# Step 4's outputs in products of 256 columns, value groups around the first new memories, and the first loads on another queue

## The chip, the cores and the metric

The kernel runs on one core of one Trainium2 chip. The metric is the device time of one execution in microseconds (us), taken as the median over runs; before the change it is 1577.51 us (three runs, 1575.53 to 1577.84). A core has engines that run side by side, each with its own instruction stream: PE (TensorE) multiplies matrices, DVE (VectorE), ACT (ScalarE) and POOL (GpSimd) work on elements, SP (SyncE) only starts transfers here. ACT and POOL can start transfers too. PE, DVE, ACT and POOL work on on-chip memory (SBUF); PE writes into accumulators (PSUM), which DVE and ACT copy out ("evict").

## The reference

Two kinds of layer, A and B, alternate twice over x, one sequence of 2048 tokens of 512 numbers:

```python
x = x + A(layernorm(x));  x = x + B(layernorm(x))
x = x + A(layernorm(x));  x = x + B(layernorm(x))

def A(x):                                # weights in bf16, 32 heads of 128
    mem = mem0                           # 8 rows of 512
    for s in range(64):                  # segments of 32 tokens
        h = concat(mem, x[32 * s: 32 * s + 32])          # 40 rows
        q, k, v = h @ Wq, h @ Wk, h @ Wv                 # per head
        p = softmax(where(mask, q @ k.T * scale, -1e9))
        o = sum over heads of (p @ v) @ Wo
        mem = o[:8]                      # the memory of the next segment
        outs.append(o[8:])

def B(x): return relu(x @ w1) @ w2       # 512 -> 1376 -> 512
```

The segments of a layer A form a chain: the memory that one segment leaves is an input of the next.

## The kernel before

**Steps.** The two A layers run interleaved. Step k works on segment k of the first A layer (called layer 0) and on segment k − 4 of the second (layer 1); DELTA is 4, and LAST is 67. Steps 0 to 3 have layer 0 only and steps 64 to 67 layer 1 only; these are called single. All weights stay in SBUF. Rows in tokens are normalized, transposed and held in xT0 (layer 0, 128 tokens a tile, by inputs_T) or xnT (layer 1 and the B layers).

**What a step does.** HT holds, transposed, the 8 memory rows and 32 tokens of each layer. A step makes queries and keys in two halves of 16 heads (qk, L610), each in three batches of 6, 6 and 4 heads (products L596; queries are evicted by ACT at L602, keys by DVE at L604). Each half goes on to the scores (L630), the softmax on DVE, ACT and POOL (L648 to L669), and the transposes of the probabilities, by PE (L678 for single steps, L690 for double ones) or by a transfer (L697). weighted_v multiplies with the values Vs (L714, L735), outputs copies the results to OTm (memory rows) and OTx (token rows). output_mem multiplies the memory rows of all heads with Wo (L638). Then new_memory (L891) follows: ACT copies the sum from PSUM into wm (L893), PE transposes it into mt (L901), and two copies put it into HTm (L912) and HT (L916). Behind it output_ride (L485) multiplies wm once more for token rows that rode along with the memory rows, and memory_values (L831) makes the values of the new memory (products L840, from HTm; ACT evicts them at L844, and they travel through DRAM into Vs).

**Values of layer 0.** They do not depend on the memory, so they are made ahead, in groups (p, n) by values0 (L300): 64 tokens (pair p of segments) by 1024 columns (n is 0, 2, 4 or 6), eight products of 512 columns (L310), one eviction (L320) into a buffer of tag "vst" (five buffers) or into a "stage" slot, which is the still empty space of w1 and w2, and one store to DRAM (L321). Later steps load them into Vs. Where the groups stand is a list: in step 0 they are written out in first_step; values_at (L879) names those of later steps, and block (L856) sets them in between the outputs; new_memory(2) takes the one of step 2.

**Outputs of tokens.** Step k's block makes the token outputs of step k − 1: output_x (L386) multiplies OTx with Wo for all heads. Where 64 rows are at hand, each head takes two products of 256 columns (halves, L377, at column places 0 and 64 of PE); in single steps, two products with even and odd heads apart (L400, four places); otherwise, with 32 rows in a double step, four products of 128 columns (L405, four places). The last form is met in step 4 alone, for the outputs of step 3. add_output (L452) adds the sums to the residual R with DVE: two additions (L383), or four of 128 columns (L470).

**Dense layers.** dense_h (L526) and dense_y (L548) make a B layer of step k − 2's rows. dense_y is cut at f_mid: the first part goes ahead of the probabilities' transposes and the rest behind them (step 3 on) or, in steps that no double step follows, behind output_mem.

**Order.** On PE, DVE, SP and POOL instructions run in the order in which the code issues them (manual_schedule, L1112). ACT's order is decided by the framework's scheduler. PSUM for queries, keys, mt, vm and transposes is a ring of three buffers (ps_c), for values and dense products one of two (ps_fill), so a late eviction holds PE up some products later. SP starts transfers in order, and a transfer that waits holds back those behind it.

**The start.** SP loads input rows 0 to 127 (load_xb(0), L107), the first half of Wq, the memory, rows 128 to 255, the first halves of Wk and Wv, and in load_rest (L142) rows 256 to 383, the second halves of the three, Wo in five parts and rows 384 to 511. POOL fills constants meanwhile, among them the zeros of P_sb, P1_sb and OTm. PE transposes the memory, then both normalized row tiles; POOL copies the tokens into HT; then step 0 begins. Step 1 loads the dense weights (load_dense, L156), normalizes rows 384 to 511 (L227) between the first key evictions and transposes them (L241) behind its memory values.

Two places set the order that the change touches: the list of groups,

```python
        if k < 5:
            return {1: [(5, 6), (7, 0), (7, 2)], 2: [(7, 4)], 4: [(7, 6)]}.get(k, [])
```

and the order of new_memory:

```python
        nc.scalar.copy(out=wm_sb[:], in_=wo[:])
        values1(k + 1, 0)
        if k == 2:
            values0(*values_at(k)[0])
        c = 1 - k % 2
        mt = ps_c.tile([128, NC4, 2, M], F32, tag="c", name="mt")
```

Of the kernel before, what the change touches and what calls it, by code (L numbers as in the profile page):

```python
# [17 lines left out]
DELTA = 4  # L18
# [4 lines left out]
def kernel(  # L23
# [80 lines left out]
    def load_xb(n):  # L104
        tag, bufs = ("vst", 5) if n in (1, 2, 3) else ("xb", 1)
        xbs[n] = wk.tile([128, Dm], BF, tag=tag, bufs=bufs, name="xb")
        nc.sync.dma_start(out=xbs[n][:], in_=A_x[0, 128 * n:128 * n + 128, :])  # L107

    load_xb(0)
    R_tiles = {}  # L110

# [24 lines left out]
    load_w(Wq_sb, Wq_v, 0)  # L136
    nc.sync.dma_start(out=mem0[0:M, :], in_=A_mem0[0, :, :])
    load_xb(1)
    load_w(Wk_sb, Wk_v, 0)
# [56 lines left out]
    P_sb = const.tile([128, 8, 128], BF)  # L196
    nc.gpsimd.memset(P_sb[:], 0.0)
    P1_sb = const.tile([128, 16 * L + 24], BF)
    nc.gpsimd.memset(P1_sb[:], 0.0)
    PT_sb = const.tile([128, 8, 2, L], BF)  # L200
# [4 lines left out]
    OTm = const.tile([128, H, 2, 6 * M], BF)  # L205
    nc.gpsimd.memset(OTm[:], 0.0)

# [91 lines left out]

    def values0(p, n, lo=0, hi=NC4, pool=None, stage=None, late=False):  # L300
        r = 64 * (p % 2)
        if (n, lo) == (0, 0):
            vd0[p] = dram.tile([4, 2, 64, 512], BF, tag="vd0", bufs=4, name="vd0")
        if lo == 0:
            pool, tag = (pool, "wo") if pool else (ps_fill, "fill")
            vp_tiles[p, n] = pool.tile([128, 512], F32, tag=tag, name="vp")
        vp = vp_tiles[p, n]
        for c4 in range(lo, hi):
            for j in range(2):
                nc.tensor.matmul(vp[64 * j:64 * j + 64, :], lhsT=xT0[p // 2][:, c4, r:r + 64],  # L310
                                 rhs=Wv_sb[:, c4, (n + j) * 512:(n + j + 1) * 512],
                                 start=(c4 == 0), stop=(c4 == NC4 - 1), tile_position=(0, 64 * j))
        if hi < NC4:
            return
        vst = wk.tile([128, 512], BF, tag="vst", bufs=5, name="vst")[:] if stage is None else stage
        if late and evict_behind:
            with tc.issue_after(evict_behind[0]):
                nc.scalar.copy(out=vst, in_=vp[:])
        else:
            nc.scalar.copy(out=vst, in_=vp[:])  # L320
        nc.sync.dma_start(out=vd0[p][n // 2].rearrange("j t e -> (j t) e"), in_=vst)  # L321
# [64 lines left out]
    def output_x(k, lo, hi):  # L386
        if not 0 <= k <= LAST or ox_span(k) is None:
            return
        r0, r1 = [x % 64 for x in (ox_span(k)[0], ox_span(k)[1] - 1)]
        r1 += 1  # L390
        if lo == 0:
            pool, tag = (ps_wo, "wo") if k < LAST else (ps_c, "c")
            wo_tiles[k] = pool.tile([128, Dm], F32, tag=tag, name="wox")
        for h in HEADS_ONE[lo:hi] if k == LAST else range(lo, hi):
            if r1 - r0 == 64:
                halves(wo_tiles[k], OTx[:, h, r0:r1], Wo_sb[:, h, :], h == 0, h == H - 1)
            elif by_heads(k):
                for j in range(2):
                    q = 32 * (2 * (h % 2) + j)
                    nc.tensor.matmul(wo_tiles[k][q:q + 32, 0:256], lhsT=OTx[:, h, r0:r1],  # L400
                                     rhs=Wo_sb[:, h, 256 * j:256 * j + 256], start=(h < 2), stop=(h >= H - 2),
                                     tile_position=(0, q))
            else:
                for j in range(4):
                    nc.tensor.matmul(wo_tiles[k][32 * j:32 * j + 32, 0:128], lhsT=OTx[:, h, r0:r1],  # L405
                                     rhs=Wo_sb[:, h, 128 * j:128 * j + 128], start=(h == 0), stop=(h == H - 1),
                                     tile_position=(0, 32 * j))
# [44 lines left out]
    def add_output(k, part=None):  # L452
# [10 lines left out]
        elif part == 1:  # L463
            return
        elif r1 - r0 == 64:
            add_halves(R[r0:r1, :], R[r0:r1, :], wo_tiles[k])
        else:
            for j in range(4):
                cs = slice(128 * j, 128 * j + 128)
                nc.vector.tensor_tensor(out=R[r0:r1, cs], in0=R[r0:r1, cs],  # L470
                                        in1=wo_tiles[k][32 * j:32 * j + 32, 0:128], op=ALU.add)
# [12 lines left out]

    def output_ride(k):  # L485
        if ride_rows(k) is None:
# [4 lines left out]
        for j in range(4):  # L491
            nc.tensor.matmul(xp[32 * j:32 * j + 32, 0:128], lhsT=sel[:, c:c + 4 * M],
                             rhs=wm_tiles[k][:, 128 * j:128 * j + 128], start=True, stop=True,
                             tile_position=(0, 32 * j))

    def add_ride(k):
# [359 lines left out]
    def block(k, lo, hi):  # L856
        output_x(k - 1, lo, hi)
        groups = values_at(k)
        if split(k):
# [4 lines left out]
            else:  # L864
                todo = [(0, 0, 2)] if lo == 0 else [(0, 2, NC4)] if hi == 16 else rest
        elif k < 5:
            todo = [(0, 0, NC4)] if k == 4 and lo else []
        else:
# [10 lines left out]
    def values_at(k):  # L879


        if k < 5:
            return {1: [(5, 6), (7, 0), (7, 2)], 2: [(7, 4)], 4: [(7, 6)]}.get(k, [])
        if k % 4 != 1 or not has0(k + 1):
# [6 lines left out]
    def new_memory(k, cont, wo):  # L891
        wm_sb = wm_tiles[k] = wk.tile([128, Dm], BF, tag="vst", bufs=5, name="wm")
        nc.scalar.copy(out=wm_sb[:], in_=wo[:])  # L893
        values1(k + 1, 0)
        if k == 2:
            values0(*values_at(k)[0])
        c = 1 - k % 2
# [16 lines left out]
        def to_queries():  # L914
            copy = nc.vector.tensor_copy if single else nc.scalar.copy
            copy(out=HT[:, :, lo:hi, 0:M], in_=mt[:, :, lo:hi, :])  # L916

        to_values()
        to_queries()

# [8 lines left out]
    def first_step():  # L929
# [5 lines left out]
        with tc.high_priority(offset=PRIO):  # L935
# [27 lines left out]
            for groups, heads in zip((((1, 4),), ((1, 6),), ((3, 4),), ((3, 6), (5, 4)), ()), WO_PARTS):  # L963
                for p, n in groups:
                    values0(p, n, stage=next(slots))
                output_mem(0, wo, *heads)
            new_memory(0, [0], wo)
            output_ride(0)
            prepare(1)

# [6 lines left out]
    def step(k):  # L977
# [9 lines left out]
        with tc.high_priority(offset=PRIO):  # L987
            behind = norm_rows.pop(k, None)
            if k == 1:
                def behind():  # L990
                    normalize(nc.vector, xbs[3], xbs[3], moments_x(3), 0, 128)
            if not single and k % 4 == 1 and has_x:
# [7 lines left out]
            if k == 1:  # L1000
                memory_values(k)
                inputs_T(3)
        part = 4 if k == LAST else 8 if single else 5
# [14 lines left out]
        def probabilities():  # L1018
# [29 lines left out]
        else:  # L1048
# [63 lines left out]
    with tc.manual_schedule(engines={mybir.EngineType.PE, mybir.EngineType.DVE, mybir.EngineType.SP,  # L1112
                                   mybir.EngineType.Pool}):
        load_rest()
        tp = transpose_pe(mem0)
        for a in range(2):
            nc.vector.tensor_copy(out=HT[:, :, a, 0:M], in_=tp[:, :, 0:M])
            nc.vector.tensor_copy(out=HTm[:, :, a * M:(a + 1) * M], in_=tp[:, :, 0:M])
        for n in range(2):
            m = moments_x(n)  # L1120
            normalize(nc.vector, xbs[n], xbs[n], m, 0, 128)
            inputs_T(n)
        load_x(0)
        nc.gpsimd.tensor_copy(out=HTm[:, :, 2 * M:32], in_=spare_T(0))
        tokens_in(0)
        first_step()
# [69 lines left out]
```

## Time and profile before

| | us |
|---|---|
| median of three runs | 1577.51 (1575.53 to 1577.84) |
| the profiled execution | 1577.01 |
| its span | 1575.1 |
| PE busy | 1545.1, 98% |
| DVE busy | 1275.4, 81% |
| ACT busy | 737.4, 47% |
| POOL busy | 349.9, 22% |

The granted clock of PE is 1.00 over the span. The span starts with the first instruction and ends with the last; the execution's own time is 1.9 us longer. PE's queue of products holds 42,803 of the kernel's 95,038 instructions, and weight loads as many again.

To read it: a line of the waits names the engine and its line, what released it, and the total, the count and the longest in us; a line of the timeline has the start, the duration, the line, the tiles and how many instructions it stands for, and in brackets the idle time before it with its releaser. "issue" means that the engine waited for nothing that the profile shows. The first two of the 40 slices (79 us) and the last are where PE is not full; steps 0 to 4 take the first 135 us or so, and a later step some 23 us ((1575 − 135) / 63).

### The profile page before, as it was taken

The page shows a single profiled execution, that of the slowest core. Times are in us where ns is not written, and L with a number is a line of the kernel's source. Part 1 is how long each engine was busy: PE and PEld are TensorE (multiplying, and loading weights), DVE is VectorE, ACT ScalarE, POOL GpSimd, SP SyncE. Part 2 cuts the span into 40 slices and gives each one's busy share as a digit, 9 for nine tenths or more (in the row PEclk, how much of TensorE's full clock was granted, in tenths as well). Part 3 has the DMA queues.
Part 4 walks back from the last instruction along what each step waited for, and adds up shares of the span by engine and source line. Part 5 has one row for each costly group of instructions (what it writes and reads, how often), then busy time and mean ns, then how long its engine had stood idle before and what let it go on. Part 6 is the DMA issues. An engine that isn't in the chain of part 4 may idle for free.

```text
span 1575.1 us, 95038 instructions
## 1 busy us (share of the span) xinstructions
PE 1545.1 (98%) x42803; PEld 1282.9 (81%) x42804; DVE 1275.4 (81%) x3300; ACT 737.4 (47%) x1778; POOL 349.9 (22%) x670
## 2 busy tenths in 40 slices
PE   5899999999999999999999999999999999999998
PEld 3577888888888888888888888888888888798876
DVE  3578888888888888888888888888888888888866
ACT  3435445454544545454454545445454544545443
POOL 2012122222222222222222222222222222222210
PEclk9999999999999999999999999999999999999999
DMA  9743342443444254343434434443433333334332
GB/s 369 247 80 71 90 83 75 86 90 84 77 92 83 74 88 92 81 78 92 83 77 84 91 83 77 93 81 81 78 91 81 76 89 77 79 81 94 74 71 43
DMA packets 222133, 146.26 MB, mean 93 GB/s; under 512 B 123576, under 2 KB 216096, under 8 KB 221728
## 3 DMA queue, kind: packets, MB, share of 16 engines
q1 hardware_dynamic: 218560, 135.96, 38.2%
q8 instruction: 336, 5.51, 1.5%
q0 software_dynamic: 3072, 4.20, 1.1%
q14 instruction: 69, 0.57, 0.1%
q10 hardware_dynamic: 96, 0.03, 0.0%
HBM read 65.41 MB, written 45.35 MB: 70 GB/s over the span
## 4 chain that ended last, share of the span: by engine, by line
PE 95%; DMA 2%; DVE 1%; SPq 1%; ACT 0%; issue 0%; POOL 0%; POOLq 0%
PE qp L596 38%; PE wox L377 10%; PE wo L638 8%; PE vm L840 7%; PE v L358 7%; PE hp L526 6%; PE sp L548 5%; PE sp L630 4%; PE vp L310 3%; PE pv L735 3%; DMA Wv_sb<-in_A_Wv_dram 2%; PE tp L690 1%; PE wox L400 1%; SPq L134 0%; PE mt L901 0%
## 5 line engine op out<-in xcount | busy, mean ns | idle before, releaser
L602 ACT CAST QT<-qp 128x480 bf16<-128x480 f32 (+3 forms) x408 | 201.7, 494 | 429.9 <-PE qp L596 429.6
L596 PE MATMUL qp<-HT,Wq_sb 128*128 128x80 bf16 (+1 forms) x8704 | 369.9, 200 | 1.7 <-POOL HT L829 1.2
L596 PEld LDWEIGHTS <-Wq_sb 128*128 128x128 bf16 x8704 | 325.3, 100 | 32.8 <-issue 25.6
L596 PE MATMUL qp<-HT,Wk_sb 128*128 128x80 bf16 (+1 forms) x8704 | 346.9, 199 | 0.7 <-DMA Wk_sb<-in_A_Wk_dram 0.7
L596 PEld LDWEIGHTS <-Wk_sb 128*128 128x128 bf16 x8704 | 319.3, 100 | 1.6 <-DMA Wk_sb<-in_A_Wk_dram 1.1
L669 POOL TENSOR_TENSOR P_sb<-es,sm 128x320 bf16<-128x320 f32 x185 | 130.8, 721 | 712.0 <-ACT QT L602 288.2
L604 DVE CAST KT<-qp 128x480 bf16<-128x480 f32 (+3 forms) x408 | 220.3, 565 | 33.2 <-PE qp L596 30.4
L648 DVE TENSOR_REDUCE mx<-sp 128x8 f32<-128x320 f32 x256 | 115.1, 487 | 133.4 <-PE sp L630 133.3
L377 PE MATMUL wox<-Wo_sb,OTx 128*64 128x256 bf16 x2880 | 173.6, 273 | 0.0
L377 PEld LDWEIGHTS <-OTx 128*64 128x64 bf16 x2880 | 150.1, 110 | 3.0
L654 ACT ACTIVATE es<-es 128x320 f32<-128x320 f32 x256 | 109.7, 469 | 61.2 <-DVE es L652 60.7
L840 PE MATMUL vm<-Wv_sb,HTm 128*32 128x512 bf16 x2176 | 129.4, 379 | 1.8 <-DVE KT L604 1.0
L638 PE MATMUL wo<-Wo_sb,OTm 128*32 128x512 bf16 x2144 | 128.6, 380 | 0.5
L358 PE MATMUL v<-Wv_sb,xnT 128*32 128x512 bf16 x2048 | 128.8, 378 | 0.0
L664 DVE TENSOR_REDUCE sm<-es 128x8 f32<-128x320 f32 x256 | 117.5, 459 | 12.9 <-ACT es L654 4.4
L622 DVE CAST sp<-maskb 128x320 f32<-128x320 bf16 x256 | 118.4, 484 | 0.0
L652 DVE TENSOR_TENSOR es<-sp,mx 128x320 f32<-128x320 f32 x256 | 113.8, 483 | 1.5
L548 PE MATMUL sp<-w_sb,hT 128*64 128x256 bf16 (+4 forms) x1452 | 104.1, 276 | 0.0
L844 ACT CAST VmS<-vm 128x512 bf16<-128x512 f32 x134 | 78.6, 587 | 44.4 <-PE vm L840 42.5
L526 PE MATMUL hp<-xnT,w_sb 128*128 128x64 bf16 (+1 forms) x2948 | 98.5, 192 | 0.6 <-DVE xnT L449 0.4
L222 POOL TENSOR_TENSOR mv<-mv,mhalf_t 128x1 f32<-128x1 f32 x82 | 45.8, 558 | 224.6 <-DVE mv L221 224.6
L840 PEld LDWEIGHTS <-HTm 128*32 128x32 bf16 x2176 | 54.6, 97 | 48.9 <-issue 3.1
(132 smaller groups left out, 2089.6 us busy)
## 6 DMA issues: line engine op xcount, KB each, us to landing
vd<-vst SPq DMA_DIRECT2D x181, 128.0 KB
Vs<-vd SPq DMA_DIRECT2D x90, 256.0 KB
vmd<-VmS SPq DMA_DIRECT2D x134, 128.0 KB
Vs<-vmd SPq DMA_DIRECT2D x254, 32.0 KB
Vs<-vmd SPq DMA_DIRECT2D x60, 128.0 KB
Wq_sb<-in_A_Wq_dram SPq DMA_DIRECT2D x2, 2048.0 KB
Wk_sb<-in_A_Wk_dram SPq DMA_DIRECT2D x2, 2048.0 KB
Wv_sb<-in_A_Wv_dram SPq DMA_DIRECT2D x2, 2048.0 KB
```

Source lines behind the costliest of these rows:

```text
L358: nc.tensor.matmul(vp[32 * j:32 * j + 32, :], lhsT=tokens[:, c4, :], rhs=Wv_sb[:, c4, n * 512:(n + 1) * 512], start=(c4 == 0), stop=(c4 == ...
L377: nc.tensor.matmul(out[64 * j:64 * j + nr, 0:256], lhsT=lhsT, rhs=rhs[:, 256 * j:256 * j + 256], start=start, stop=stop, tile_position=(0, ...
L526: nc.tensor.matmul(hp[:, fc - f0, 0:n], lhsT=w1_sb[:, c4, u:u + 128], rhs=cols(c4), start=(c4 == 0), stop=(c4 == NC4 - 1))
L548: nc.tensor.matmul(sp_banks[bank][64 * j:64 * j + n, 0:w], lhsT=hT_tiles[d][0:fs, fc, 0:n], rhs=w2_flat[0:fs, fc * Dm + 256 * j:fc * Dm + ...
L596: nc.tensor.matmul(qp[:, hi, 0:ncol], lhsT=W_sb[:, c4, h * Dh:(h + 1) * Dh], rhs=HT[:, c4, a_lo:a_hi, :], start=(c4 == 0), stop=(c4 == NC4 ...
L602: nc.scalar.copy(out=dst[:, 0:nh, a_lo * L:a_hi * L], in_=qp[:, 0:nh, 0:ncol])
L604: nc.vector.tensor_copy(out=dst[:, 0:nh, a_lo * L:a_hi * L], in_=qp[:, 0:nh, 0:ncol])
L622: nc.vector.tensor_copy(out=sp_tiles[a], in_=maskb2)
L638: nc.tensor.matmul(wo[32 * j:32 * j + 32, :], lhsT=OTm[:, h, n, 2 * M * c:2 * M * c + 4 * M], rhs=Wo_sb[:, h, :], start=(h < 4), stop=(h > ...
L664: nc.vector.tensor_reduce(out=sm[:], in_=es[:], axis=AX.X, op=ALU.add)
L669: eng.tensor_tensor(out=P, in0=es[:], in1=sm[:].unsqueeze(2).to_broadcast([128, 8, L]), op=ALU.mult)
L840: nc.tensor.matmul(vp[32 * j:32 * j + 32, :], lhsT=HTm[:, c4, :], rhs=Wv_sb[:, c4, n * 512:(n + 1) * 512], start=(c4 == 0), stop=(c4 == NC ...
```

## The change

It has these parts:

1. Input rows 0 to 127, the memory and rows 128 to 255 are loaded by ACT's queue; SP's queue begins with the first half of Wq.
2. Rows 0 to 127 are normalized, transposed and copied into HT before the memory's transposes and copies; rows 128 to 255 come behind those. The zeros of P_sb, P1_sb and OTm are written by POOL behind its first copies.
3. A table, around, gives new_memory(0) and new_memory(1) one value group each: six of its eight products stand between the copy of wm and mt, the last two in output_ride. Group (5, 6) moves from step 1's block to step 0, (7, 4) from new_memory(2) to step 1's block, (7, 6) from step 4's block to step 1's new memory. In step 0, (5, 4) is evicted by DVE.
4. new_memory(0) copies HT before HTm; the other steps keep HTm first.
5. In step 1 the normalizing of rows 384 to 511 moves behind the memory values, and their transposes into the second half's queries and keys, behind the first batch.
6. In step 2 f_mid is 7 instead of 6: dense_y has 14 products in its first part and 8 in its second.
7. Step 4 makes step 3's outputs with halves: 64 products of 256 columns instead of 128 of 128, and two additions instead of four. No value group is left in step 4.

Its core:

```diff
     def load_xb(n):
...
-        nc.sync.dma_start(out=xbs[n][:], in_=A_x[0, 128 * n:128 * n + 128, :])
+        queue = nc.scalar if n < 2 else nc.sync
+        queue.dma_start(out=xbs[n][:], in_=A_x[0, 128 * n:128 * n + 128, :])
     load_xb(0)
+    nc.scalar.dma_start(out=mem0[0:M, :], in_=A_mem0[0, :, :])
+    load_xb(1)
...
     load_w(Wq_sb, Wq_v, 0)
-    nc.sync.dma_start(out=mem0[0:M, :], in_=A_mem0[0, :, :])
-    load_xb(1)
...
-            if r1 - r0 == 64:
+            if r1 - r0 == 64 or k == DELTA - 1:
                 halves(wo_tiles[k], OTx[:, h, r0:r1], Wo_sb[:, h, :], h == 0, h == H - 1)
...
-        elif r1 - r0 == 64:
+        elif r1 - r0 == 64 or k == DELTA - 1:
             add_halves(R[r0:r1, :], R[r0:r1, :], wo_tiles[k])
...
+    around = {0: (5, 6), 1: (7, 6)}
-    def output_ride(k):
+    def output_ride(k, stage=None):
...
+        if k in around:
+            values0(*around[k], 3, NC4, stage=stage)
...
-        elif k < 5:
-            todo = [(0, 0, NC4)] if k == 4 and lo else []
...
-            return {1: [(5, 6), (7, 0), (7, 2)], 2: [(7, 4)], 4: [(7, 6)]}.get(k, [])
+            return {1: [(7, 0), (7, 2), (7, 4)]}.get(k, [])
...
         values1(k + 1, 0)
-        if k == 2:
-            values0(*values_at(k)[0])
+        if k in around:
+            values0(*around[k], 0, 3)
...
+        if k == 0:
+            to_queries()
         to_values()
-        to_queries()
+        if k:
+            to_queries()
...
-                    values0(p, n, stage=next(slots))
+                    values0(p, n, stage=next(slots), by_vector=(p, n) == (5, 4))
...
-            output_ride(0)
+            output_ride(0, next(slots))
...
-            if k == 1:
-                def behind():
-                    normalize(nc.vector, xbs[3], xbs[3], moments_x(3), 0, 128)
...
             if k == 1:
                 memory_values(k)
-                inputs_T(3)
+                normalize(nc.vector, xbs[3], xbs[3], moments_x(3), 0, 128)
...
             if k == 1:
+                inputs_T(3)
                 load_dense()
...
-        f_mid = 9 if not single else 6 if ahead or k == 2 else 5
+        f_mid = 9 if not single else 6 if ahead else 7
...
         load_rest()
+        m = moments_x(0)
+        normalize(nc.vector, xbs[0], xbs[0], m, 0, 128)
+        inputs_T(0)
+        tokens_in(0)
         tp = transpose_pe(mem0)
         for a in range(2):
             nc.vector.tensor_copy(out=HT[:, :, a, 0:M], in_=tp[:, :, 0:M])
             nc.vector.tensor_copy(out=HTm[:, :, a * M:(a + 1) * M], in_=tp[:, :, 0:M])
-        for n in range(2):
-            m = moments_x(n)
-            normalize(nc.vector, xbs[n], xbs[n], m, 0, 128)
-            inputs_T(n)
+        m = moments_x(1)
+        normalize(nc.vector, xbs[1], xbs[1], m, 0, 128)
+        inputs_T(1)
+        nc.gpsimd.tensor_copy(out=HTm[:, :, 2 * M:32], in_=spare_T(0))
+        nc.gpsimd.memset(P_sb[:], 0.0)
         load_x(0)
-        nc.gpsimd.tensor_copy(out=HTm[:, :, 2 * M:32], in_=spare_T(0))
-        tokens_in(0)
+        nc.gpsimd.memset(P1_sb[:], 0.0)
+        nc.gpsimd.memset(OTm[:], 0.0)
         first_step()
```

More of the change, by code (lines that the diff above doesn't have):

```diff
@@ L196 @@
     P_sb = const.tile([128, 8, 128], BF)
-    nc.gpsimd.memset(P_sb[:], 0.0)
     P1_sb = const.tile([128, 16 * L + 24], BF)
-    nc.gpsimd.memset(P1_sb[:], 0.0)
     PT_sb = const.tile([128, 8, 2, L], BF)
@@ L205 @@
     OTm = const.tile([128, H, 2, 6 * M], BF)
-    nc.gpsimd.memset(OTm[:], 0.0)
     sp_banks, sp_tiles = [], []
@@ L298, with values0 @@
     evict_behind = []
-    def values0(p, n, lo=0, hi=NC4, pool=None, stage=None, late=False):
+    def values0(p, n, lo=0, hi=NC4, pool=None, stage=None, late=False, by_vector=False):
         r = 64 * (p % 2)
@@ L319, in values0 @@
         else:
-            nc.scalar.copy(out=vst, in_=vp[:])
+            (nc.vector.tensor_copy if by_vector else nc.scalar.copy)(out=vst, in_=vp[:])
         nc.sync.dma_start(out=vd0[p][n // 2].rearrange("j t e -> (j t) e"), in_=vst)
```

## The prediction

> **What bounds the kernel now.** First the totals and slices of the page:
>
> ```profile
> PE 1545.1 (98%) x42803; PEld 1282.9 (81%) x42804; DVE 1275.4 (81%) x3300; ACT 737.4 (47%) x1778; POOL 349.9 (22%) x670
> ...
> PE   5899999999999999999999999999999999999998
> ...
> PE 95%; DMA 2%; DVE 1%; SPq 1%; ACT 0%; issue 0%; POOL 0%; POOLq 0%
> ```
>
> PE (matmul) is busy 98% of the span and carries 95% of the chain that ended last. Its idle time, 30 us, lies at the two ends; the only thin slices are the first two and the last. So PE's waits of the first 160 us come next (total, times, longest):
>
> ```profile
> PE wox L405 <- issue: 1.5, 1, 1.5
> ...
> PE mt L901 <- ACT wm L893: 1.4, 2, 0.7
> ...
> PE vm L840 <- DVE KT L604: 1.0, 1, 1.0
> ...
> PE qp L596 <- DMA Wk_sb<-in_A_Wk_dram: 0.7, 1, 0.7
> PE vf L332 <- DMA Wv_sb<-in_A_Wv_dram: 0.6, 1, 0.6
> PE qp L596 <- DVE HT L916: 0.5, 1, 0.5
> ```
>
> For 160 to 1500 us the same view has no line. From step 5 on, the change leaves every engine's order as it is, so only these stretches count. PE's timeline places them (start, duration, idle before in brackets):
>
> ```profile
> 32.51 0.77 PE L596 MATMUL qp<-HT,Wk_sb 128*128 128x40 bf16 x24 [0.66 <-DMA Wk_sb<-in_A_Wk_dram]
> ...
> 37.68 1.91 PE L332 MATMUL vf<-Wv_sb,HT 128*40 128x512 bf16 x16 [0.58 <-DMA Wv_sb<-in_A_Wv_dram]
> ...
> 50.83 0.27 PE L901 MATMUL mt<-sel,wm 128*32 128x16 bf16 x16 [0.69 <-ACT wm L893]
> ...
> 51.64 0.77 PE L596 MATMUL qp<-HT,Wq_sb 128*128 128x40 bf16 x24 [0.47 <-DVE HT L916]
> ...
> 56.03 1.91 PE L840 MATMUL vm<-Wv_sb,HTm 128*32 128x512 bf16 x32 [1.02 <-DVE KT L604]
> ...
> 88.37 0.71 PE L548 MATMUL sp<-w_sb,hT 128*32 128x256 bf16 x10
> 89.01 1.05 PE L310 MATMUL vp<-Wv_sb,xT 128*64 128x512 bf16 x8
> 90.00 0.27 PE L901 MATMUL mt<-sel,wm 128*32 128x16 bf16 x16
> ...
> 123.69 1.08 PE L405 MATMUL wox<-Wo_sb,OTx 128*32 128x128 bf16 x64
> 126.29 0.80 PE L405 MATMUL wox<-Wo_sb,OTx 128*32 128x128 bf16 x44 [1.52 <-issue]
> 127.02 1.05 PE L310 MATMUL vp<-Wv_sb,xT 128*64 128x512 bf16 x8
> ```
>
> The reader is to see that up to 37.7 us a weight transfer fixes PE, whatever ran before it; later each hole has a name.
>
> **The change part by part.** The sum stands against the profiled run (1577.01 us, span 1575.1), which is 0.50 below the median 1577.51.
>
> Early loads and start order. Input rows 0 and the memory leave SP's queue for ACT's; the first weight half is issued by SP at 0.81 instead of 1.28, so all weight transfers move up by at most 0.47. Normalizing rows 0 before the memory's transposes and moving three POOL memsets (0.95, 0.65, 2.66 us) behind the first copies let the first products start earlier than 16.38. But everything before 32.51 and 37.68 waits for Wk's and Wv's second half: what is won there only lengthens those two waits. Gain 0.4; ends: 0.5 (the issue times) and a loss of 0.3 (the DMA engines moved 273, 90, 287, 254 and 410 GB/s in the half microseconds from 2.0 on, so three small transfers in parallel could take as much as SP's turn gave).
>
> Step 0's end. Six products of group (5,6) go between the copy of the new memory and its transposes (mt), two behind. Eight take 0.98, so six take 0.74, beside a wait of 0.69: 0. If ACT's copy were later they would still be cover; if it came sooner, they would cost up to 0.74, but its source ends at 50.14. HT is now copied by DVE before ACT's HTm. DVE's copy ran 51.39–51.58; it can now start where ACT's did, 51.17: −0.22 (0 to −0.3). The two last products and their eviction go beside that wait. The eviction of (5,4) by DVE instead of ACT delays nothing that PE waits for: 0. One more store on SP ahead of step 1's value loads: 0 with 7 us to spare (loads at 54.95, first use at 66.16).
>
> Step 1. DVE's statistics and normalizing of rows 3 stood between two key evictions (from 53.41 to 55.65, where the last of it waits for POOL); the third key eviction, and with it the buffer for vm (L840), came late. Moved behind the evictions it frees PE: −1.02 (−0.6 if half of the wait becomes one for ACT's Q eviction, which ends at 55.39). Behind the normalizing now stand DVE's first score reductions; it needs 2.24 us and PE's vm takes 1.84, the scores 0.3: at most 0.1, on a path with cover. The transposes of rows 3 (0.33) are only moved: 0. In new_memory(1), group (7,6) fills 0.73 and 0.34 of waits: 0. Step 1's block swaps (5,6) for (7,4): 0.
>
> Step 2. The buffer of the second memory-value eviction is freed by the store of (7,0), which now stands behind the dense loads (2.75 MB, issued 60.65 to 64, traffic to 71.5). ACT takes that eviction behind two Q evictions of step 2; the third Q batch needs its PSUM buffer, at 74.86 + 0.59 = 75.46 against 75.31: +0.15 (0 to +0.3). SP's row behind it moves by some 2.2 us and the transposed rows still come 0.7 ahead of L526 at 81.43. Group (7,4) goes from 89.01: mt is then set by ACT's copy, 88.59 + 0.59 + 0.05 = 89.23, instead of 90.00: −0.77 (−0.4 if the copy slips), leaving a hole of 0.35. Two dense products ahead of the softmax's transposes shorten a wait of 0.45 there: 0.
>
> Step 4. Group (7,6) goes: −0.98. The outputs of step 3 take 64 products of 256 columns for 128 of 128. Before: 0.40 + 1.00 + 0.73 = 2.13 of products and 1.52 of waiting, 3.65. After: the rows with the same two column places are L377 (64 wide, 54 from 170.74 to 173.79, 56 ns) and L548 (32 wide, ten from 88.37 to 89.01, 64 ns). Between them I take 60: 64 × 60 = 3.84, +0.19 with the stall gone. Far ends: 32 ns of L400, which uses four places (2.05, so −1.6), and 66 (4.2, +0.55). Two additions of 256 columns on DVE instead of four of 128 (1.18 together) are off the path: 0.
>
> Why the stall goes. No engine is named for it, and one 16 KB packet of an instruction queue lies in 119–120, 123–124 and 127–128. PE's 85,607 instructions over that queue's 336 packets are 255 each, so one packet is a page. Ahead of the stall, from 121.95 to 124.77, run 140 products and their weight loads, 280 instructions: more than a page in 2.8 us, while pages come some 4 us apart. The new form issues 128 instructions in 3.84 us, a third of the old rate, so a page lasts longer than its successor takes to come.
>
> The Trainium skill ("Runtime: NRT & Kernel Launch", section "Instruction fetch mechanics") says that the sequencer fetches the next page while it runs the current one, and that a crossing is mostly hidden. By that rule the stall would not be the instructions' and could stay; the trace's 1.52 beside a packet speaks against "hidden" here.
>
> Sum: −0.4 − 0.22 − 1.02 + 0.15 − 0.77 − 0.98 + 0.19 = −3.05, so 1577.01 − 3.05 = **1574.0**.
>
> **The rivals.**
>
> B, the early loads bring nothing: the last half of Wv lands no sooner, since 16 engines at 410 GB/s to 40 us, not the issue, set it. For it: the rate; against: SP's first issue does start earlier. 1574.4.
>
> C, the 1.52 us wait stays, at step 4 or at another dense stretch of steps 0 to 4, because only the page's end has moved. For it: other stretches as quick as L405 remain (32 scores from 123.18 to 123.69, 16 ns each). Against: no other such wait in the trace. 1573.96 + 1.52 = 1575.5.
>
> D, the earlier start leaves PE idle longer, some 2 us, ahead of Wk's half, and the products after it run slow. Rows: 24 products of 40 columns took 0.80 at 16.38 after idling and 0.62 at 32.51. The 120 products ahead of 35.37 at that rate cost 0.9: 1574.9. Against: 0.66 of idling at 32.51 slowed nothing. The Trainium skill ("TensorE: Matmul & The Clock Gate", section "HAM oscillation — how this bites in real kernels") puts the limit at idle gaps of about 3.4 us, which 2 us would not reach; the trace's 16.38 follows gaps of 2.61, 1.56 and 1.21, so it neither proves nor denies that.
>
> E, slower. PE issues 128 instructions fewer before step 5, half a page, so in steps 5 to 67 all page ends fall elsewhere. Place: a page that ends in the quickest steady stretch, transposes and weighted values from 174.90 to 176.55, 84 products and so 168 instructions in 1.65 us. Price: one wait of 1.52 for every four steps, 16 × 1.52 = 24, 1598. Two such waits take the gain away (3.05 / 1.52), five make it slower by more than the bound ((1580.7 − 1574.0) / 1.52 = 4.4). Against: over 300 page ends already went by with no wait from 160 to 1500, and 256 instructions from 174.90 on take until about 179, 4 us, as long as a page takes to come.
>
> **How the numbers follow.** A 0.58, B 0.10, C 0.13, D 0.07, E 0.12. A's own range is 1573.0 to 1576.1: the terms' favourable ends give −3.6, the others −0.9, and the runs spread by 2.3. A measurement can tell about 0.2% (3.2 us) from no change: faster means below 1574.35, and 1574.0 lies just under it. A gives two thirds to faster, B half, C and D little: 0.38 + 0.05 + 0.04 = 0.47. Slower is E and a remainder of A to D: 0.13. Same: 0.40. The range leaves out E and the far end of L400's row: 1572.6 to 1577.0.
>
> **What would show it.** Right: no wait of vm for KT in step 1; mt waits for wm once, some 0.35, in step 2; a new wait of about 0.15 for an eviction of VmS in step 2; no wait of issue at wox in step 4, and 64 of its products at 56 to 64 ns; longer waits for Wk's and Wv's second halves, with Wv's products starting at about 37.3; no wait from step 5 on and the span from there unchanged. Wrong: a wait of 1.5 us at any dense stretch, above all one that repeats every four steps; products slower than 25 ns ahead of 35 us; the dense loads holding up SP so far that L526 waits in step 2.

## The result and the profile after

The changed kernel takes 1579.68 us (median of 22 runs, 1576.97 to 1581.63) against 1577.28 for the kernel before in the same comparison (22 runs, 1575.53 to 1578.53): a ratio of 1.0016, with a 95% interval of 1.0009 to 1.0022. It is 2.4 us slower, where 3.5 us less had been forecast. Its profiled execution took 1578.38 with a span of 1576.7, somewhat below its median.

The page's totals, slices and chain of the changed kernel look like those of before, and nothing in them tells where the time went:

```profile
span 1576.7 us, 94912 instructions
...
PE 1549.1 (98%) x42740; PEld 1286.2 (82%) x42740; DVE 1276.6 (81%) x3299; ACT 736.4 (47%) x1777; POOL 349.3 (22%) x670
...
PE   6999999999999999999999999999999999999998
...
PE 96%; DMA 2%; DVE 1%; issue 0%; ACT 0%; SPq 0%; POOL 0%; POOLq 0%; ACTq 0%
```

PE has 64 products fewer (63 by the page, where a record can be missing) and is nevertheless busy 4.0 us longer. PE's waits of the first 160 us in the changed kernel (total, times, longest):

```profile
PE qp L598 <- DMA Wk_sb<-in_A_Wk_dram: 3.9, 2, 2.4
...
PE qp L598 <- issue: 1.4, 2, 0.9
...
PE vm L842 <- DVE KT L606: 0.4, 1, 0.4
...
PE mt L901 <- ACT wm L893: 0.3, 1, 0.3
```

The waits that the change aims at are gone or shrunk: mt for wm from 1.4 to 0.3, vm for KT from 1.0 to 0.4, and the wait of 1.52 for no engine at step 4's outputs. In their place stand longer waits for Wk, as forecast, and new waits for no engine ("issue") in the queries, keys and dense products of step 2, which were not. PE's timeline shows them, and the new form of step 4's outputs:

```profile
72.69 0.39 PE L598 MATMUL qp<-HT,Wq_sb 128*128 128x40 bf16 x9 [0.85 <-issue]
...
80.15 0.19 PE L598 MATMUL qp<-HT,Wk_sb 128*128 128x40 bf16 x1 [0.54 <-issue]
...
84.43 0.83 PE L550 MATMUL sp<-w_sb,hT 128*32 128x256 bf16 x11 [0.40 <-issue]
...
89.33 0.27 PE L901 MATMUL mt<-sel,wm 128*32 128x16 bf16 x16 [0.26 <-ACT wm L893]
...
123.15 3.12 PE L375 MATMUL wox<-Wo_sb,OTx 128*32 128x256 bf16 x54
126.11 1.18 PE L550 MATMUL sp<-w_sb,hT 128*32 128x320 bf16 x18
```

To find the rest, one marks the same instruction in each step, the first product of mt, and compares its starts. In steps 4 and 66 of the kernel before:

```profile
133.39 0.27 PE L901 MATMUL mt<-sel,wm 128*32 128x16 bf16 x16
...
1546.95 0.27 PE L901 MATMUL mt<-sel,wm 128*32 128x16 bf16 x16
```

and of the changed kernel:

```profile
131.49 0.27 PE L901 MATMUL mt<-sel,wm 128*32 128x16 bf16 x16
...
1548.53 0.27 PE L901 MATMUL mt<-sel,wm 128*32 128x16 bf16 x16
```

At step 4 the changed kernel is 1.90 ahead. From there to step 66 it takes 1417.04 where before took 1413.56: 3.48 more, with the same instructions in the same order on every engine. This difference is called the late loss below. It is not spread evenly: 45 of the 62 steps last as long as before to 0.02 us, 12 last 0.1 to 1.0 longer, and one is 0.37 shorter. From 160 to 1500 us, where the view of before has no line, PE's waits in the changed kernel are:

```profile
PE qp L598 <- issue: 1.3, 4, 0.7
PE hp L528 <- DMA xnT<-XN: 0.2, 1, 0.2
```

They hold less than half of the late loss. One place shows why, in the changed kernel's timeline of PE:

```profile
1106.66 0.56 PE L632 MATMUL sp<-KT,QT 128*40 128x40 bf16 x32
1107.15 0.93 PE L598 MATMUL qp<-HT,Wq_sb 128*128 128x80 bf16 x21
1108.28 0.28 PE L598 MATMUL qp<-HT,Wq_sb 128*128 128x80 bf16 x3 [0.20 <-issue]
1108.39 1.03 PE L598 MATMUL qp<-HT,Wk_sb 128*128 128x80 bf16 x24
1109.25 0.92 PE L598 MATMUL qp<-HT,Wq_sb 128*128 128x80 bf16 x21
```

24 such products normally start 0.86 apart, 36 ns each (1108.39 to 1109.25); so the 22nd was due at 1107.91 and came at 1108.28, 0.37 late. The bracket shows only 0.20 of it, because the end of the products ahead of it is modelled; so the starts are what to compare. No engine and no transfer is named. The DMA queues in the microsecond ahead, from 1106 to 1107:

```profile
DMA packets 436, 0.15 MB, mean 147 GB/s; under 512 B 400, under 2 KB 435, under 8 KB 435
...
q1 hardware_dynamic: 435, 0.13, 306.7%
q8 instruction: 1, 0.02, 7.6%
...
Vs<-vmd SPq DMA_DIRECT2D x3, 32.0 KB
```

The last column is the time that the packets took as a share of all 16 engines' time; 306.7% means that about three were under way on each engine at once. One 16 KB packet of PE's instruction queue (q8) goes there, among the packets of the step's value loads. PE goes on about a microsecond after its end.

### The profile page after: what moved, and what is told of

It reads as the page before. It is cut to its first block, busy times and chain, and to the rows that moved or that the text cites. A ratio compares the mean times of both kernels' runs of the same rounds, so it can differ in the third digit from the quotient of the medians.

```text
span 1576.7 us, 94912 instructions
## 1 busy us (share of the span) xinstructions
PE 1549.1 (98%) x42740; PEld 1286.2 (82%) x42740; DVE 1276.6 (81%) x3299; ACT 736.4 (47%) x1777; POOL 349.3 (22%) x670
## 4 chain that ended last, share of the span: by engine, by line
PE 96%; DMA 2%; DVE 1%; issue 0%; ACT 0%; SPq 0%; POOL 0%; POOLq 0%; ACTq 0%
PE qp L598 39%; PE wox L375 10%; PE wo L640 8%; PE vm L842 7%; PE v L356 7%; PE hp L528 6%; PE sp L550 5%; PE sp L632 4%; PE vp L308 3%; PE pv L737 3%; DMA Wk_sb<-in_A_Wk_dram 2%; PE tp L692 1%; PE wox L398 1%; PE mt L901 0%; DMA xnT<-XN 0%
## 5 line engine op out<-in xcount | busy, mean ns | idle before, releaser
L375 PE MATMUL wox<-Wo_sb,OTx 128*64 128x256 bf16 (+1 forms) x2944 | 177.5, 274 | 0.0
L375 PEld LDWEIGHTS <-OTx 128*64 128x64 bf16 (+1 forms) x2944 | 153.2, 110 | 3.3
```

The source lines that it names most:

```text
L375: nc.tensor.matmul(out[64 * j:64 * j + nr, 0:256], lhsT=lhsT, rhs=rhs[:, 256 * j:256 * j + 256], start=start, stop=stop, tile_position=(0, ...
```

## The experiments

Each ratio below is against runs of the kernel before on the same chip; the medians of before in the five comparisons were 1576.75 to 1578.42.

**Theory P.** The change takes 128 instructions (64 products and their weight loads) from PE ahead of step 5. PE's instructions come in packets of 256, the pages of the prediction (here 85,480 products and weight loads in 335 packets, 255 each). So every later packet ends half a packet away from where it ended before. In the trace of before three steps of four have about 1299 instructions on PE (5 × 256 + 19) and the fourth has 1219 (5 × 256 − 61), so the packet ends move on by 19 three times and then back by 61: from step 5 to step 63 they stay, within some 100 instructions, at the same five places of a step. A shift of 128 puts them at other places for all of steps 5 to 67. **Rival R.** Another part of the change has a lasting effect on transfers or buffers.

### Padding only

Tiny products at the start move the packet ends and nothing else. All other engines' instructions are the same, in number and order. The padding also takes a PSUM buffer of ps_fill, but the kernels with 128 and with 256 instructions take the same one.

```diff
+    def pad(n):
+        idle = ps_fill.tile([128, Dm], F32, tag="fill", name="idle")
+        for i in range(n):
+            nc.tensor.matmul(idle[0:32, 0:16], lhsT=ident[:, 0:32], rhs=ident[:, 0:16], start=True, stop=True)
...
         load_rest()
+        pad(64)
```

> The changed kernel with 64 tiny products (32 rows, 16 columns, into an unused accumulator) added to PE right after its first two products, that is 128 PE instructions with their weight loads, in a wait of 1.8 us. PE's stream then stands in steps 5 to 67 where it stood in the kernel before, to one instruction, and every other engine's order is that of the changed kernel. Theory P (the place of the page ends among PE's instructions sets the loss after step 5): no waits of 0.1 us and more at the second half's first products, the gain of 1.9 us at step 5 is kept, about 1575.3 (1574.5 to 1576.3). Rival R (the loss comes from another part of the change, which shifts transfers or buffers for good): like the changed kernel, about 1579.7 (1578.7 to 1580.7).

> The changed kernel with 128 tiny products, 256 PE instructions, a whole page, at the same place: the control for the padding itself. Theory P: page ends fall as in the changed kernel, so about 1579.7 (1578.5 to 1581.0), with waits at the second half's first products. If the padding helps in another way (a warmer clock, a later start), it would be near 1575.3 like the kernel with 128 instructions. Rival R: 1579.7 as well.

> The kernel before with 64 tiny products, 128 PE instructions, in its wait of 3.9 us at the start and nothing else changed. Theory P: it gets the changed kernel's page ends in steps 5 to 67, so it loses the 3.8 us that the changed kernel's trace lost there, less the 0.6 that the trace of before lost: about 1580.7 (1579.5 to 1582.5). Rival R: unchanged, 1577.3 (1576.5 to 1578.0).

Measured: the changed kernel with 128 instructions more, 1577.06, ratio 1.0000 (0.9991 to 1.0009); with 256 more, 1580.45, 1.0023 (1.0014 to 1.0032); the kernel before with 128 more, 1584.49, 1.0047 (1.0034 to 1.0059). Half a packet takes the loss away from the changed kernel and brings it, larger, to the kernel before; a whole packet does nothing. That settles for P against R, and rules out that the padding, or its buffer, helps by itself. PE's waits from step 5 on, in the kernel before with half a packet of padding:

```profile
PE qp L596 <- issue: 3.5, 8, 0.7
```

For the unpadded kernel before the same view has no line. Two sizes were off. The first kernel was expected at 1575.3 and came at 1577.06: its profile ends step 0 1.2 later than before (1.3 later than the changed kernel) and has "issue" waits of 1.0, 0.7 and 0.5 in steps 0 to 4, whose packet ends it moves too. The third lost more than the 3.4 expected: its late loss is 6.1, and 1.3 were lost up to step 4.

That the waits lie at packet ends can also be counted. Number all of PE's recorded instructions, weight loads included, from the start: the three waits of step 2 in the changed kernel come after 2241, 2753 and 3009 of them, 512 and 256 apart, and the wait of 1.52 in step 4 of the kernel before after 5313, which is 10 × 256 more than 2753. In all 16 profiles the waits for no engine in steps 0 to 4, 43 of 0.14 us or more, come after a multiple of 256 plus 193, so always at the same place of a packet.

### Step 4's form

The changed kernel with the old form of step 4, which has the 128 instructions back without any padding:

```diff
-            if r1 - r0 == 64 or k == DELTA - 1:
+            if r1 - r0 == 64:
...
-        elif r1 - r0 == 64 or k == DELTA - 1:
+        elif r1 - r0 == 64:
```

> The changed kernel with the old form of step 4's outputs (128 products of 128 columns, four additions) and all else changed. It has 128 PE instructions more than the changed kernel, so that the page ends of steps 5 to 67 are those of before to one instruction. Theory P: no late waits; step 4 has the old wait of up to 1.5 us if the page ends there as before (then 1576.8), otherwise about 1575.3: range 1574.8 to 1577.3. Rival R: the loss is not in step 4's form, so 1579.7 or, with the old wait, up to 1581.2.

Measured 1575.69, ratio 0.9992 (0.9983 to 1.0000), 4.8 us below the changed kernel with a whole packet of padding on the same chip. Its profile, 1.8 below the kernel's median, still has a wait of 1.2 at step 4's outputs, and a late loss of 0.24. The other way round, the kernel before with the new form alone (the two lines above reversed):

> The kernel before with step 4's outputs as 64 products of 256 columns and two additions alone: 128 PE instructions fewer, nothing else changed (the value group stays in step 4). Theory P: the wait of 1.5 in step 4 goes, but from step 5 on the page ends are those of the changed kernel, whose profile lost 3.4 between steps 4 and 66 against before; 5.0 and 5.9 were lost by the two kernels with a page or half a page of padding. So slower by 2 to 4.5 (about +3). As predicted for this part alone: +0.19 - 1.52 + 1.33 of forecast form cost, about 0.

Measured 1582.18, ratio 1.0032 (1.0019 to 1.0044). The edit that only shortens PE's stream and takes its wait of 1.52 away makes the kernel 5.2 us slower, more than the 2 to 4.5 expected. Its mt starts in steps 4 and 66:

```profile
133.85 0.27 PE L901 MATMUL mt<-sel,wm 128*32 128x16 bf16 x16
...
1552.18 0.27 PE L901 MATMUL mt<-sel,wm 128*32 128x16 bf16 x16
```

1418.33 apart, a late loss of 4.77. Step 4 itself lasts 24.45 instead of 24.61. It nevertheless ends 0.46 behind, with "issue" waits of 0.69 and 0.53 in step 2, where before has one of 0.28. Up to step 4 both kernels run the same instructions, so this much differs from one execution to the next with the packet ends in the same places.

### A quarter of a packet and three quarters

The padding of the kernel before with 32 and with 96 products:

> The kernel before with 32 tiny products, 64 PE instructions, in the wait of 3.9 us at the start. Theory P: a quarter page moves the page ends by half the way that half a page does. In before the five page ends of a step enter at PE instructions 105 to 206, 357 to 462, 613 to 718, 869 to 974 and 1125 to 1230 of it; with half a page more at 233 to 334 and 997 to 1102, the two places where the packets came too late. With 64 they enter at 41 to 142, 293 to 398, 549 to 654, 805 to 910 and 1061 to 1166, so that a part of the steps is at those two places: between before and the kernel with half a page, 1 to 5 slower. If any padding at the start costs the same, 7.7 slower; if only half a page does, 0.

> The kernel before with 96 tiny products, 192 PE instructions, in the wait at the start. The page ends of a step then enter at about 169 to 270, 421 to 526, 677 to 782, 933 to 1038 and 1189 to 1294. Reading Z1 (the loss needs page ends at 260 to 334, ahead of the second half's first products, where the packets share the queues' traffic): none but the last few steps, so 0 to +0.7 late. Reading Z2 (it needs them at 997 to 1102, ahead of the transposes and weighted values, where PE runs through a page's instructions in 2.5 us): two in five steps, +1.5 to +2.5 late. Steps 0 to 4 add -1 to +1.5 either way, as in the other padded kernels.

Measured 1579.44, 1.0016 (1.0007 to 1.0025), and 1580.63, 1.0017 (1.0009 to 1.0026): both between before and the kernel with half a packet. Their late losses are 1.92 and 1.30. In the second, the two longest waits from 160 to 1500 us, of 0.32 each, are again at the second half's first products and none is at the transposes and weighted values. That speaks against reading Z2 but is no proof of Z1: the late loss of 1.30 lies between the 0 to 0.7 of Z1 and the 1.5 to 2.5 of Z2, and the profiled run is 0.4 below the kernel's median.

### The same change with its instructions put back elsewhere

64 tiny products in waits of steps 1 and 2 (40 and 24), the same with four column places for step 4's outputs, and 64 products of 64 columns in the wait for Wk's second half:

```diff
+            if k == 1:
+                pad(40, ps_wo, "wo")
             if single:
                 transpose_one(act[0])
...
+        if k == 2:
+            pad(24, ps_fill, "fill")
         c = 1 - k % 2
```

> The changed kernel with 64 tiny products (128 PE instructions) in waits of steps 1 and 2: 40 ahead of the probabilities' transposes of step 1, 24 ahead of mt in step 2. Page ends are the changed kernel's up to step 1 and those of before, to one instruction, from step 3 on. Theory P: no late loss, and step 4 without its wait of 1.2 to 1.5 us that the kernel with the old form of step 4 still shows: about 1574.5 (1573.5 to 1575.7), some 1.2 below the kernel with the old form (1575.7) and 5 below the changed kernel. Rival Q (the gain of the old form came from that form and not from the number of instructions): about 1579.7 less at most 0.5.

```diff
-            elif by_heads(k):
+            elif by_heads(k) or k == DELTA - 1:
...
-        if by_heads(k) and r1 - r0 == 32:
+        if (by_heads(k) or k == DELTA - 1) and r1 - r0 == 32:
```

> The same kernel with the products of step 4's outputs at four column places instead of two (even and odd heads apart, as the single steps have them; again 64 products of 256 columns, 128 instructions, and four additions). Rows: 16 of these took 0.55 us at 75.71 in the changed kernel, 34 ns each, against 56: 64 x 34 = 2.2 for 3.6, so 1.4 less than its sister with waits in steps 1 and 2: about 1573.1 (1572.3 to 1574.5) if PE gets its instructions in time; about 1574.5, no gain, if the quicker stretch brings a wait for them of 1.2 to 1.5 us in step 4.

```diff
+            def between():
+                values0(5, 0, stage=next(slots))
+                pad(64, ps_wo, "wo", 64)
```

> The changed kernel with 64 products of 32 rows and 64 columns (128 PE instructions) in the wait of 2.4 us for Wk's second half in step 0. Page ends from there on are those of before to one instruction, and PE doesn't stand idle there for over 2 us. Theory P: about 1575.0 (1574.0 to 1576.5). Theory D (the idle time there halves the granted clock for 3.4 us, as the changed kernel's records show from 31.95 on): no drop of the clock near 32 us, the products ahead of Wv's second half end 0.3 to 0.6 us earlier, so that PE waits for Wv there again. Against D: the clock drops all the same, or the end of step 0 does not come earlier than at 50.3 to 50.7.

Measured: 1577.61, 0.9996 (0.9986 to 1.0005); 1577.91, 0.9998 (0.9989 to 1.0007); 1578.28, 1.0001 (0.9992 to 1.0010). All three lose the changed kernel's 0.16% and none gains what was expected. In the first, the padding in step 1 was not free (the transposes behind it start 1.1 later within the step than in its sister with padding in step 0), and its profile has a late loss of 2.96, with one "issue" wait of 0.6, although its packet ends are those of before to one instruction: the right place makes the waits rarer, it does not exclude them. In the second the four-place products of step 4 do run quicker, 52 in 1.43 us (127.96 to 129.39, 27 ns each), but there are two waits of 0.22 ahead of and within them, and its profiled run was its slowest, 1582.11, with the clock halved three times. In the third PE was busy without a break from 28 to 34 us, and the clock stayed at 1.00: 24 products of Wk's second half take 0.61 (33.36 to 33.97) where the changed kernel took 0.81 (32.11 to 32.92). That agrees with theory D but is no clean test of it: with the old form of step 4 and no padding there, the wait ahead was only 0.65, and the 24 products took the same 0.61 (32.02 to 32.63). And in the padded kernel they start 1.25 later, the half clock came at 20 to 24 us instead, a wait of 1.27 for no engine stands at 39.00, and step 0 ended at 52.57 instead of 50.73.

### The early start

The old start (SP's queue, memory first, POOL's zeros first) under the changed kernel with step 4's old form; the new start on the kernel before; the old start under the changed kernel:

```diff
-        queue = nc.scalar if n < 2 else nc.sync
-        queue.dma_start(out=xbs[n][:], in_=A_x[0, 128 * n:128 * n + 128, :])
+        nc.sync.dma_start(out=xbs[n][:], in_=A_x[0, 128 * n:128 * n + 128, :])
...
-    nc.scalar.dma_start(out=mem0[0:M, :], in_=A_mem0[0, :, :])
-    load_xb(1)
...
     load_w(Wq_sb, Wq_v, 0)
+    nc.sync.dma_start(out=mem0[0:M, :], in_=A_mem0[0, :, :])
+    load_xb(1)
```

> The changed kernel with the old form of step 4 and, in addition, the old start: loads of rows 0, the memory and rows 128 on SP's queue, memory first, POOL's zeros first. It prices the early loads alone, at equal page ends from step 1 on. Forecast as predicted: 0.4 slower than the kernel with the old form alone (1575.7), so 1576.1. Rival: nothing is gained by them, since the last half of Wv or the slower clock after the longer idle time takes the gain away: 1575.7 or up to 0.3 less.

> The kernel before with the change's early loads and start order alone. PE's stream from step 0's first products on is that of before, to one instruction. As predicted: 0.4 faster, 0 to 0.5. Theory D (starting earlier only makes PE idle longer ahead of three weight halves, and the granted clock is then halved for 3.4 us or more in places that differ from run to run): 0.5 to 1.5 slower, with one or two stretches at half clock between 16 and 36 us of the span, and a step 0 that ends between 50.3 and 52.6.

> The changed kernel with the old start (loads on SP's queue, memory first, POOL's zeros first) and all else changed, so page ends as in the changed kernel. As predicted for the early loads: 0.4 slower than the changed kernel, ratio to before 1.0018. If the early start costs as in the two comparisons so far (+1.0 alone, +1.4 on the kernel with the old form of step 4): 1.0008 (1.0002 to 1.0014).

Measured: 1575.90, 0.9984 (0.9975 to 0.9993); 1577.96, 1.0004 (0.9995 to 1.0013); 1580.95, 1.0021 (1.0013 to 1.0030). Against their sisters (0.9992, 1.0000 and 1.0016) the early start comes out at +0.0008, +0.0004 and −0.0005: no effect that these runs can tell from none. What speaks for a cost in single runs is the clock. The windows of the changed kernel (busy time and count of PE, PEld, DVE, ACT and POOL, then the granted clock, the DMA share and GB/s):

```profile
28.00:30.00 2.00, 1.71 (x33) 0.98 (x32) 0.00 (x0) 1.20 (x3) 0.00 (x0) 1.00 1.03 369
30.00:32.00 2.00, 0.00 (x0) 0.00 (x0) 0.00 (x0) 0.33 (x1) 0.00 (x0) 0.99 1.03 410
32.00:34.00 2.00, 1.89 (x57) 1.89 (x58) 0.41 (x1) 0.02 (x1) 0.00 (x0) 0.50 1.02 408
34.00:36.00 2.00, 1.94 (x65) 1.80 (x62) 1.03 (x3) 0.56 (x2) 0.00 (x0) 0.66 1.03 384
```

Toward the end of a wait of 2.40 for Wk, which lasts to 32.11, the clock is halved, from 31.95 to 35.36. The new start alone shows the same at another place:

```profile
18.00:20.00 2.00, 0.52 (x8) 0.34 (x10) 1.17 (x3) 0.47 (x1) 0.00 (x0) 1.00 1.07 354
20.00:22.00 2.00, 2.00 (x14) 0.94 (x12) 0.99 (x3) 0.88 (x2) 0.00 (x0) 0.57 1.02 404
22.00:24.00 2.00, 2.00 (x20) 0.56 (x20) 1.18 (x2) 0.28 (x1) 0.00 (x0) 0.58 1.02 410
24.00:26.00 2.00, 2.00 (x30) 0.98 (x24) 1.18 (x5) 1.17 (x2) 0.64 (x2) 1.00 1.03 410
```

It nevertheless ended step 0 at 50.24, 0.6 ahead of before: the half clock lay beside the waiting for weights.

### One part of step 1

```diff
-            if k == 1:
-                def behind():
-                    normalize(nc.vector, xbs[3], xbs[3], moments_x(3), 0, 128)
...
                 memory_values(k)
-                inputs_T(3)
+                normalize(nc.vector, xbs[3], xbs[3], moments_x(3), 0, 128)
...
             if k == 1:
+                inputs_T(3)
                 load_dense()
```

> The kernel before with the normalizing of rows 384 to 511 behind the memory values and their transposes in the second half, alone. No PE instruction more or fewer before step 2 and none moved by more than a batch. As predicted: 1.0 faster (0.6 to 1.0), PE's wait of vm for KT in step 1 gone. If what stands behind it in step 1 takes the place of the wait, 0.

Measured 1576.31, 0.9996 (0.9987 to 1.0005), 0.65 below before. From mt of step 0 to mt of step 1 its profile takes 18.36 where before took 19.07, so 0.71 was gained, and vm's wait for KT is gone.

### A version that beats both

The changed kernel with the old form of step 4 and the old start, thus parts 3 to 6 of the change and step 4 without its value group, has the best ratio, 0.9984 (0.9975 to 0.9993), 2.5 us below before on the same chip. Its packet ends are those of before, and from 160 to 1500 us PE's waits have no line; its late loss is 0.84.

The late losses of all profiles, one execution of each kernel, from the mt starts in steps 4 and 66, stand by where the packet ends fall:

| packet ends in steps 5 to 67 | late loss, us |
|---|---|
| as before (the kernel before, and eight others) | 0, 0.24, 0.32, 0.62, 0.84, 1.15, 1.17, 1.23, 2.96 |
| a quarter or three quarters on | 1.92, 1.30 |
| half a packet on (the changed kernel, and four others) | 3.48, 4.21, 4.77, 5.10, 6.11 |

The groups do not overlap but for the 2.96 of the kernel with padding in steps 1 and 2, for which no run gives the reason.

## Why the prediction was wrong

**The step that failed** is the sentence that from step 5 on the change leaves every engine's order as it is, "so only these stretches count". The order is the same, but not the place of PE's packet ends, and the term for steps 5 to 67, which the sum has at zero, measured +3.5 in the changed kernel's profile and +4.8 in that of step 4's form alone. Rival E named this mechanism, half a page's shift for all later steps, and was given 0.12. What it had wrong was the place and the price. It looked at the quickest stretch, the transposes and weighted values, and took each wait at 1.52. The waits are at the second half's first queries and keys, where a packet travels beside the value loads, and they cost 0.1 to 0.9. They fall in one step of six or so, and mostly in other steps in each of the five profiles with these packet ends; the changed kernel's runs spread over 4.7 us where before spreads over 3.0, which fits. Its evidence against itself, that over 300 page ends went by without a wait from 160 to 1500 us (the trace of before has 291 packets there), was the wrong inference: as the ends stay within some 100 instructions of the same places, they are only five places of a step, seen nearly sixty times each.

The Trainium skill ("Runtime: NRT & Kernel Launch", section "Instruction fetch mechanics") has the crossing of such a block as mostly hidden. The trace agrees for most crossings, and for nearly all at the places of before; at the places of the changed kernel the rest cost 3.5 us.

**Step 4.** The form's price was right: the 54 products start 123.15 and the next work 126.11, 2.96 or 55 ns each, where 60 was taken and 56 was the near end. The value group's 0.98 is saved. Step 4 lasts 23.36 instead of 24.61 from mt to mt, 1.25 less where 0.79 was forecast. That the wait of 1.52 belongs to PE's instructions shows in its count (5313, above) and in the old form's later profiles: with the same 128 products it was 1.4, 1.2, 0.9, 0.4 and 0.3 in five of them, and absent in two, the version that beats both and the kernel before with half a packet of padding.

**Steps 1 and 2.** vm's wait was sized at 1.02 with 0.6 as the lower end; measured 0.71 alone, and 0.36 of wait stays. The mt hole was 0.26 for 0.35. Rival C, the same kind of wait at another dense stretch, came true three times over in the changed kernel's step 2: 0.85, 0.54 and 0.40, 1.79 in all. This is most of why its gain at step 4 is 1.90 and not 3.05: from mt to mt, step 1 gained 1.03 of the 1.24 forecast, and step 2 lost 0.46 where 0.62 of gain was forecast. How much of it one execution pays is chance in part: step 2 with the packet ends of before cost 0.28 in the profile of before and 1.22 in that of step 4's form alone. The other versions show such waits at other places of steps 0 to 4.

**The start.** All weight waits moved as forecast (Wv's products start at 37.34, forecast 37.3). But step 0 ended only 0.09 earlier: the products ahead of Wv ran at half clock. So rival D was right in that profile, where slow products followed the longer wait. The falls of the clock came with waits of 2.40 here, and of 1.50 and 1.48 in the profiles of the old form of step 4 and of the new start alone, all below the 3.4 that the prediction held against D; but a wait of 1.60 in the kernel before with half a packet of padding brought none. In the runs neither D nor the 0.4 can be told from nothing.

What stays open: why the waits from step 5 on come ahead of a packet's end and not at it, by the count above up to 52 instructions in the changed kernel and 74 in the kernel before with half a packet of padding; and why the packet is late there. The traces show that it starts late rather than travels slowly: in the nine steps from step 5 on where the changed kernel lost 0.1 or more at these products, it took 1.0 to 1.3 us, where the median of all is 1.07, but it started 1.1 to 2.0 after PE had passed the end of a packet, where the median is 0.7. Whether the value loads cause that, no run shows; none took them away.

## What to carry to other kernels

Where one engine is busy 98% of the time and its stream is long and periodic, the number of instructions ahead of the periodic part is a parameter of its own: here half a packet of 256 was worth 2.5 to 8 us in 1577, as much as the best version gained or more. Before an edit early in such a kernel is judged by its time, give its instruction count back (or pad to the old count modulo 256) and compare again; an edit that "only removes instructions" can lose. The kernel with padding in steps 1 and 2 warns that the old count does not bring the old time back in every case. And compare step by step on a fixed mark, since a loss that is spread over a few of sixty steps shows in no total of the page.

## What the runs showed that was not expected

- 64 unused products of 16 columns at the start, in a wait of 3.9 us, make the kernel before 0.47% slower (0.34 to 0.59).
- The granted clock of PE fell to 0.50 near the waits for weights of step 0 in six profiles, at different places between 20 and 38 us, for 3.4 us in five and 6.8 in one; in that one, the kernel with four column places, it did so also from 68.8 to 72.2 and from 133.6 to 137.0 us, when PE had been busy for 2.5 and 2.1 of the 3.4 us before.
- The waits for instructions have no releaser in the profile and are partly hidden by the modelled ends of the products ahead: 0.20 in the bracket for 0.37 in the starts.
